# Emptying a PSUM bank before the score copies, and one P@V visit for tiles that span two batches

## The chip, the core and the metric

The kernel runs on one core of one Trainium2 chip. The metric is the device time of one execution in microseconds (us); the median of several runs counts. The engines are called as the profile calls them: PE (TensorE's matmuls) with PEld (its weight loads), DVE (VectorE), ACT (ScalarE), POOL (GpSimd) and SP (SyncE, which here only issues DMAs).

## What is computed

Attention in which each query keeps its 32 largest scores, and behind it a feed-forward layer with the activation h cos h:

```python
# q, k, v: (8 batches, 8 heads, 576 tokens, 64)
scores = scale * np.matmul(q, k.transpose(0, 1, 3, 2))
kth = np.partition(scores, -32, axis=-1)[..., -32:-31]
scores = np.where(scores >= kth, scores, -1e9)
scores = scores - np.max(scores, axis=-1, keepdims=True)
attn = np.exp(scores)
attn = attn / (np.sum(attn, axis=-1, keepdims=True) + 1e-09)
x = np.matmul(attn, v)          # then as (4608 tokens, 512)
h = x @ w_in                    # w_in: 512 x 2048
out = (h * np.cos(h)) @ w_out   # w_out: 2048 x 512
```

All of it is float32.

## The kernel before

**Tiles, units, slots, blocks.** The 4608 tokens are cut into 36 tiles of 128. A tile with one pair of heads is a *unit*; four pairs make 144 units, four for each tile. As a batch has 576 tokens, that is 4.5 tiles, four of the tiles (the fifth of each nine) span two batches: 64 of their rows belong to one batch and 64 to the next, and they need the k and v of both. The main loop has one *slot* for each unit (`slot`, L724), and each engine's instructions are written in the order in which the slots are written. I call the slots of a *block* (the four of a tile) slot 0 to slot 3, after i mod 4.

**One unit's way.** It is a software pipeline. Scores are made by PE one or two slots ahead, in slots 0 and 2 for two units each (`scores`, L229): 448 columns into a bank `sc`, the last 128 into parts of a shared PSUM tile `rim`. ACT copies both parts to SBUF (`take_scores`, L246 and L250). In slot i, DVE folds the row of unit i in two halves (L258), with POOL making the lower half (L274, L283), and searches the top 32 (L350 MAX8, L355 MATCH_REPLACE8). In slot i + 1 the bounds of this search (L363, L370) go to ACT, which masks (L377, L379) and takes exponentials (L387, with the denominators accumulated); DVE sums and inverts the denominators (L395, L400). In slot i + 2 POOL splits the weights into 16-bit halves (L410, L412), and SP writes them to DRAM (`rows`, L438) and reads them back transposed (`pT`, L444).

**P@V.** `values` (L469) multiplies pT by v into `rim`, for several units in one *visit*. Which slot has the visit of which unit is set by `value_slot` (L672). An ordinary tile has one visit for its four units, in slot 2 of the next block. A spanning tile has two visits: units 0 and 1 in slot 0 of the next block, units 2 and 3 in slot 2. After a visit DVE multiplies by the inverted denominators and writes xT (`take_values`, L481). xT, L250 and P@V all touch `rim`, and L250 in a slot with a visit waits for the visit's end, as xT waits for that L250.

**Feed-forward.** `ff1` (L530) is the input projection: eight items for a block, and two of them, a *pair*, fill one PSUM bank (`mm`). ACT empties a full bank twice, into g (L544) and x (L546); POOL reduces the argument (L566, L575), ACT takes the sine (L585, with its own table load), POOL multiplies (`gate`, L592). `ff2` (L605) is the output projection, eight items that all add up in one other bank; ACT empties it (L615) and sends it out. The two banks `mm` are the only ones, so with the output projection in one, all pairs go through the other in turn.

**The order by hand.** `plan` (L717) says for each of the four slots which feed-forward items come at its three feeds (0 is an ff1 item, 1 an ff2 item): the first feed stands before the scores and P@V of the slot, the second and third behind. `take_banks` (L552) writes the emptying of the banks that are complete by then, where it is called; in a slot this was between the mask and the exponentials (L758), and again behind the second feed (L773). The block's first pair of ff1 items is in slot 3: with the plan before, its first item is in the first feed and its second in the second feed.

**Loads.** SP issues the loads of q, k and v. `load_at` (L690) puts at most one load in a slot, at the earliest in the slot where the last reader of its buffer stands. The pool `loads` has six buffers each for q, k and v.

Of the kernel before, what the change touches and what calls it, by code (L numbers as in the profile page):

```python
# [10 lines left out]
F32 = mybir.dt.float32  # L11
# [6 lines left out]
P = 128  # L18
# [12 lines left out]
def kernel(  # L31
# [13 lines left out]
    NT = S // P  # L45
    TAIL = S - NT * P
    MAIN = NT * P
    NP = H // 2
# [6 lines left out]
    consts = ctx.enter_context(tc.tile_pool(name="consts", bufs=1))  # L55
    loads = ctx.enter_context(tc.tile_pool(name="loads", bufs=6))
    work = ctx.enter_context(tc.tile_pool(name="work", bufs=2))
    small = ctx.enter_context(tc.tile_pool(name="small", bufs=4))
    ps = ctx.enter_context(tc.tile_pool(name="ps", bufs=2, space=bass.MemoryType.PSUM))
    dram = ctx.enter_context(tc.tile_pool(name="dram", bufs=4, space=bass.MemoryType.DRAM))  # L60
    ffw = ctx.enter_context(tc.tile_pool(name="ffw", bufs=2))
# [41 lines left out]
    def load_weights(n, queue):  # L103
        for _ in range(n):
            i = wq["next"]
            if i >= len(chunks):
                return
            src, dst = chunks[i]
            if not DECODE:
                queue.dma_start(out=dst, in_=src)  # L110
                wq["next"] = wq["done"] = i + 1
                continue
            spare = i < 2 * NC + 10 and i % 2 == 1 and staged(1) < XB
            if spare:
                st = ffw.tile([P, CW, 2], I32, tag="x", name="st", bufs=XB)
            elif staged() + ff["live"] >= CHUNKS:
                return
            else:
                st = ffw.tile([P, CW, 2], I32, tag="g", name="st", bufs=CHUNKS)
            queue.dma_start(out=st.rearrange("p w i -> p (w i)"), in_=src)  # L120
            wq["loaded"].append((st, dst, int(spare)))
            wq["next"] = i + 1
# [16 lines left out]
    def decode_second(n):  # L139

        for _ in range(min(n, len(wq["second"]))):
            st, w, spare = wq["second"].popleft()
            wi = w.bitcast(I32)
            nc.vector.tensor_scalar(
                out=wi, in0=wi, scalar1=3, scalar2=None, op0=ALU.logical_shift_left
            )
            wq["third"].append((st, w, spare))
# [14 lines left out]
    for t0 in range(0, B * S, P):  # L162
        parts = []
# [14 lines left out]
    def place(hp, j):  # L178

        return (hp + j) % 2  # L180
# [23 lines left out]
    def load_v(b, hp):  # L204
        st = pairs.setdefault((b, hp), {})
        cols = slice(hp * P, (hp + 1) * P)
        t = loads.tile([P, NT, P], F32, tag="v", name="v")
        nc.sync.dma_start(out=t, in_=v[b, 0:MAIN, cols].rearrange("(c p) e -> p c e", p=P))
        st["v"] = t

        t = st["v_tail"] = v_tails[b % 2 * NP + hp]
        for j in range(2):
            nc.sync.dma_start(
                out=t[place(hp, j) * TAIL : (place(hp, j) + 1) * TAIL],
                in_=v[b, MAIN:S, hp * P + j * D : hp * P + (j + 1) * D],
            )
# [61 lines left out]
    def fold_low(u):  # L278

        if u["n"] in BUSY:  # L280
            return
        low = u["low"].bitcast(I32)
        nc.gpsimd.tensor_tensor(  # L283
            out=low, in0=low, in1=u["rest"][:, :, HS:S].bitcast(I32), op=ALU.subtract
        )

    dens = []
    for i in range(3):
        t = consts.tile([P, 2, 2], F32, tag=f"dens{i}", name=f"dens{i}")
        nc.vector.memset(t[:, :, 1], EPS)  # L290
        dens.append(t)

    tops = []
    for i in range(3):
        t = consts.tile([P, 2, TOPK + 1, 2], F32, tag=f"top{i}", name=f"top{i}")
        nc.vector.memset(t[:, :, 0, 1], -NEG)
        tops.append(t)
# [3 lines left out]
    def topk_first(u, w):  # L301

        u["top"] = tops[u["n"] % len(tops)]
        if w:
            merge_first(w)
        if u["n"] not in BUSY:
            fold_sum(u)
        fold_high(u)
        if w:
            merge_second(w)  # L310
        if u["n"] in BUSY:
            fold_now(u)
        topk_round(u, 0, [lambda: bounds(w), lambda: distances(w)] if w else ())

    def topk_round(u, rnd, between=(), ahead=None):
        top, rest, lasts = u["top"], u["rest"], TOPK // 8 - 1
        end = TOPK - 1 - 8 * rnd
        at = top[:, :, end : end - 8 if rnd < lasts else None : -1, 0]
        search(
            at, rest[:, :, HS:S] if rnd == 0 else rest[:, :, 0:HS], rest[:, :, 0:HS], rnd < lasts,  # L320
            between if rnd < lasts else (),
        )
        if rnd < lasts:
            return
        del u["rest"]
        low = u.pop("low")
        for k in range(TOPK // 16):
            more = k < TOPK // 16 - 1
            if ahead and not more:
                take_values(ahead)  # L330
            search(top[:, :, 1 + 8 * k : 9 + 8 * k, 1], low, low, more, () if more else between)
# [51 lines left out]
    def exponentials(u):  # L383
        s, nd = u["s"], u.pop("nd")
        den = u["den"] = dens[u["n"] % len(dens)]
        for j in range(2):
            nc.scalar.activation(  # L387
                out=s[:, j], in_=s[:, j], func=AF.Exp, bias=nd[:, j : j + 1], scale=SCALE,
                accum_out=den[:, j, 0:1],
            )  # L390
# [57 lines left out]
    def place_of(u):  # L448

        bank, at = u["hp"] % 2, u["hp"] // 2 * P  # L450
        return bank, room[bank][:, at : at + P]
# [23 lines left out]
    def take_values(us):  # L475
        blk, hp, n = block_of[us[0]["tok"]], us[0]["hp"], len(us)
        if "xT" not in blk:
            blk["xT"] = work.tile([P, NP, P], F32, tag="xT", name="xT", bufs=3)
        for i, u in enumerate(us):
            to, o, pT = blk["xT"][:, hp + i], place_of(u)[1], u.pop("pT")  # L480
            nc.vector.tensor_tensor(out=to, in0=o, in1=pT[:, 2 * NT + 1], op=ALU.mult)  # L481
        blk["left"] -= n
        blk["tick"] = ff["tick"]
# [5 lines left out]
    for w in widths:  # L489
        blk = {"t0": t0, "w": w, "left": 0, "g": [], "gated": []}  # L490
# [61 lines left out]
    def take_banks():  # L552
        while full:
            take, *what = full.popleft()
            take(*what)
# [116 lines left out]
    def value_slot(i, u):  # L672

        if i < NP:
            return NP + 1
        return i - i % NP + NP + (0 if len(u["parts"]) == 2 and u["hp"] < 2 else 2)

    valued = {}
    for i, u in enumerate(units):
# [1 line left out]
    scored, last, last_values = {}, {}, {}  # L681
# [8 lines left out]
    def load_at(i, *what):  # L690
        while i in at_slot:
            i += 1
        at_slot[i] = what

    order = [(b, hp) for b in range(B) for hp in range(NP)]
    for n in range(NP, len(order)):
        i = last[order[n - 6]] if n >= 6 else 0
        load_at(max(i, 2 * NP + 2), load_qk, *order[n])
        i = last_values[order[n - 6]] if n >= 6 else 0
        load_at(max(i, 2 * NP + 2), load_v, *order[n])  # L700

    for hp in range(NP):
# [8 lines left out]
    def send(x):  # L711
# [6 lines left out]
        ((0, 0), (1,), (1,)),  # L718
        ((0, 0), (1, 1), (0,)),
        ((0,), (1,), ()),  # L720
        ((1, 0), (0, 1), (1,)),
    )

    def slot(i, u, w, x, z):  # L724
        n = (3, 4, 4, 4, 4, 3)[i] if i < NP + 2 else 2
        if i < NP:
            for load, b, hp in at_once[i]:
                load(b, hp)
        load_weights(n, nc.sync if i < NP + 2 else nc.scalar)
        if x:  # L730
            (turn if i < NP + 2 else send)(x)
        decoding = i < 3 * NP
        ff["late"] = False
        topk_first(u, w)
        fold_low(u)
        topk_round(u, 1)
        topk_round(u, 2)
        if i > 0:
            decode_second(NP)
            decode_third()  # L740
        reduce_first()
        reduce_second()
        made = scored.get(i, [])
        if z:
            take_banks()
        feed(*plan[i % NP][0])

        for m in made:
            scores(m)
        if z:  # L750
            values(z)


        if i % 2 or decoding:
            sines(1)
        if w:
            mask(w)
        take_banks()  # L758
        if w:
            exponentials(w)  # L760
        if i + 1 < NU:
            take_scores(units[i + 1])
        topk_round(u, 3, both(w), z)
        if i == 0:
            decode_second(NP)
            decode_third()
        ff["late"] = True
        if i in at_slot:
            load, b, hp = at_slot[i]
            load(b, hp)  # L770
        gate(1)
        feed(*plan[i % NP][1])
        take_banks()  # L773
        decode_first(NP)
        reduce_first()
        reduce_second()
        feed(*plan[i % NP][2])
# [40 lines left out]
    for i in range(NU):  # L818
        ff["now"] += 1
        wq["ready"] = wq["done"]  # L820
        u, w, x = (units[i - n] if n <= i else None for n in range(3))
# [46 lines left out]
```

## Time and profile before

| | |
|---|---|
| median of 3 runs (lowest, highest) | 1444.02 us (1443.61, 1445.5) |
| profiled execution | 1442.98 us |
| its span, first to last instruction | 1441.2 us |
| mean granted PE clock, whole span | 0.984 |
| PE, DVE, POOL, ACT busy | 95%, 94%, 81%, 76% |
| HBM traffic | 101 GB/s |

How to read the views. The page gives the busy time of each engine and, as digits, its busy share in 40 equal slices. The timeline lists instructions by their start: start, duration, engine, line, operation, what is written from what, how many equal ones follow each other, and in brackets the engine's idle time before them with what ended it. A row of matmuls in float32 counts two records for each matmul; their ends are modelled, so for PE starts are compared with starts. A window line gives busy times of the engines in a stretch. Before 110 us the granted PE clock was 0.83, from 280 us on it was 1.00. The weights are decoded in the first 110 us.

### The profile page before, as it was taken

The page shows a single profiled execution, that of the slowest core. Times are in us where ns is not written, and L with a number is a line of the kernel's source. Part 1 is how long each engine was busy: PE and PEld are TensorE (multiplying, and loading weights), DVE is VectorE, ACT ScalarE, POOL GpSimd, SP SyncE. Part 2 cuts the span into 40 slices and gives each one's busy share as a digit, 9 for nine tenths or more (in the row PEclk, how much of TensorE's full clock was granted, in tenths as well). Part 3 has the DMA queues.
Part 4 walks back from the last instruction along what each step waited for, and adds up shares of the span by engine and source line. Part 5 has one row for each costly group of instructions (what it writes and reads, how often), then busy time and mean ns, then how long its engine had stood idle before and what let it go on. Part 6 is the DMA issues. An engine that isn't in the chain of part 4 may idle for free.

```text
span 1441.2 us, 30374 instructions
## 1 busy us (share of the span) xinstructions
PE 1376.0 (95%) x10304; PEld 993.1 (69%) x10304; DVE 1352.8 (94%) x5235; ACT 1091.4 (76%) x1922; POOL 1167.5 (81%) x804
## 2 busy tenths in 40 slices
PE   5558999999999999999999999999999999999998
PEld 3446677777777767777777767777777776777775
DVE  8999999999999999999999999999999999999931
ACT  7877777777877777778777787877777778777741
POOL 4878888888888887888888888888888888888820
PEclk9688999999999999999999999999999999999999
DMA  9576766566665566556665666657666566565630
GB/s 296 181 217 175 185 190 173 151 170 188 163 176 148 160 187 171 167 146 194 171 187 141 143 185 182 173 139 186 187 162 165 151 170 155 151 160 148 154 99 15
DMA packets 427437, 240.02 MB, mean 167 GB/s; under 512 B 375952, under 2 KB 392592, under 8 KB 427280
## 3 DMA queue, kind: packets, MB, share of 16 engines
q1 hardware_dynamic: 420720, 224.22, 57.8%
q10 hardware_dynamic: 6560, 13.85, 2.7%
q8 instruction: 81, 1.33, 0.4%
q14 instruction: 76, 0.62, 0.1%
HBM read 45.09 MB, written 101.19 MB: 101 GB/s over the span
## 4 chain that ended last, share of the span: by engine, by line
PE 63%; ACT 19%; DVE 16%; issue 1%; POOL 1%; POOLq 0%
PE mm L530 26%; PE o L605 18%; PE rim L469 10%; PE sc L236 7%; DVE top L350 7%; ACT s L387 4%; ACT L387 3%; ACT s L379 3%; ACT s L246 2%; DVE rest L355 2%; DVE rest L258 2%; DVE xT L481 2%; PE rim L236 2%; ACT x L546 2%; ACT s L250 2%; ACT g L544 1%
## 5 line engine op out<-in xcount | busy, mean ns | idle before, releaser
L530 PEld LDWEIGHTS mm<-xT,w_in 128*128 128x128 f32 x4608 | 535.8, 192 | 97.4 <-issue 49.1
L530 PE MATMUL mm<-xT,w_in 128*128 128x128 f32 x4608 | 543.5, 276 | 18.0 <-ACT x L546 14.6
L605 PE MATMUL o<-w_out,g 128*128 128x512 f32 x1152 | 524.7, 599 | 0.0
L350 DVE MAX8 top<-rest 128x8 f32<-128x288 f32 x1152 | 478.8, 451 | 0.0
L355 DVE MATCH_REPLACE8 rest<-top,rest 128x288 f32<-128x288 f32 x864 | 376.5, 443 | 0.0
L605 PEld LDWEIGHTS o<-w_out,g 128*128 128x128 f32 x1152 | 207.7, 190 | 217.8 <-issue 210.5
L410 POOL COPY halves<-s 128x2304 uint16<-128x2304 uint16 x140 | 294.8, 2106 | 76.0 <-ACT s L387 75.9
L350 DVE MAX8 top<-low 128x8 f32<-128x288 f32 x576 | 241.8, 448 | 0.6 <-POOL low L283 0.6
L387 ACT ACTIVATE s<-s,nd 128x576 f32<-128x576 f32 x288 | 220.4, 769 | 0.8
L283 POOL TENSOR_TENSOR low<-low,rest 128x576 int32<-128x576 int32 x141 | 199.4, 1414 | 11.1
L379 ACT ACTIVATE s<-s,top 128x576 f32<-128x576 f32 x288 | 205.6, 761 | 0.0
L274 POOL TENSOR_TENSOR low<-s 128x576 int32<-128x576 int32 x141 | 199.0, 1411 | 6.0 <-ACT s L250 6.0
L377 ACT ACTIVATE nd<-nd 128x2 f32<-128x2 f32 x144 | 29.4, 204 | 207.0 <-DVE nd L370 207.0
L575 POOL TENSOR_TENSOR x<-g,x 128x1024 f32<-128x1024 f32 x68 | 161.2, 2371 | 5.7
L592 POOL TENSOR_TENSOR g<-g,x 128x1024 f32<-128x1024 f32 x68 | 160.9, 2366 | 0.0
L236 PE MATMUL sc<-k,q 64*128 64x448 f32 (+1 forms) x640 | 148.7, 587 | 11.6 <-DMA k<-in_k_dram 6.2
L469 PE MATMUL rim<-pT,v 128*64 128x128 f32 (+1 forms) x2560 | 139.9, 267 | 0.0
L469 PEld LDWEIGHTS rim<-pT,v 128*64 128x64 f32 x2560 | 129.7, 139 | 7.1 <-issue 6.0
L246 ACT COPY s<-sc 128x896 f32<-128x896 f32 x144 | 128.3, 891 | 3.2 <-PE sc L236 3.1
L355 DVE MATCH_REPLACE8 low<-top,low 128x288 f32<-128x288 f32 x288 | 125.4, 443 | 0.0
L544 ACT ACTIVATE g<-mm 128x512 f32<-128x512 f32 x144 | 85.4, 593 | 48.1 <-PE mm L530 47.6
L258 DVE TENSOR_TENSOR rest<-sc,s 128x576 f32<-128x576 f32 x144 | 107.8, 749 | 10.5 <-ACT s L250 10.3
(54 smaller groups left out, 1236.1 us busy)
## 6 DMA issues: line engine op xcount, KB each, us to landing
rows<-halves SPq DMA_DIRECT2D x140, 640.0 KB, 3.0
out_dram<-ob ACTq DMA_DIRECT2D x36, 256.0 KB, 2.1
q<-in_q_dram SPq DMA_DIRECT2D x31, 288.0 KB, 3.5
st<-in_moe_w_in_dram SPq DMA_DIRECT2D x16, 512.0 KB, 6.1
v<-in_v_dram SPq DMA_DIRECT2D x32, 256.0 KB, 3.2
k<-in_k_dram SPq DMA_DIRECT2D x31, 144.0 KB, 3.3
k<-in_k_dram SPq DMA_DIRECT2D x32, 128.0 KB, 3.6
st<-in_moe_w_out_dram SPq DMA_DIRECT2D x8, 512.0 KB, 4.3
```

The lines of the kernel that those rows point to most:

```text
L236: nc.tensor.matmul(to[r0 : r0 + rows, rim_bank(r0, j) if k0 else place(u["hp"], j), 0 : k1 - k0], st["q"][d, q0 : q0 + rows], st["k"][d, k ...
L274: nc.gpsimd.tensor_tensor(out=u["low"].bitcast(I32), in0=s[:, :, 0:HS], in1=s[:, :, HS:S], op=ALU.add)
L283: nc.gpsimd.tensor_tensor(out=low, in0=low, in1=u["rest"][:, :, HS:S].bitcast(I32), op=ALU.subtract)
L350: nc.vector.max(to[:, j], src[:, j])
L355: nc.vector.match_replace(rest[:, j], to[:, j], src[:, j], NEG)
L379: nc.scalar.activation(out=s[:, j], in_=s[:, j], func=AF.Prelu, bias=less[:, j, 1:2], scale=1.0, alpha=FAR)
L387: nc.scalar.activation(out=s[:, j], in_=s[:, j], func=AF.Exp, bias=nd[:, j : j + 1], scale=SCALE, accum_out=den[:, j, 0:1],)
L410: nc.gpsimd.tensor_copy(out=halves[:, :, 0 : 2 * S], in_=s.rearrange("p (k h) -> p h k", h=2))
L469: nc.tensor.matmul(to[d, r], lhsT, rhs, start=(bank, j) not in begun, stop=c == NT - 1 and u in us[-2:] and r0 + rows == P,)
L530: nc.tensor.matmul(mm[:, at : at + w], w_in[f // FC][:, c, (f % FC) * P : (f % FC + 1) * P], blk["xT"][:, c], start=c == 0, stop=c == NC - 1,)
L575: nc.gpsimd.tensor_tensor(out=x, in0=g, in1=x, op=ALU.subtract)
L605: nc.tensor.matmul(o, g[:, at : at + P], w_out[f], start=f == 0, stop=f == NF - 1)
```

## The change

Nothing is computed differently. The plan gives both items of a block's first pair to the first feed of slot 3, and the two output items behind them to the second feed. In slot 3, banks are no longer emptied between the mask and the exponentials, but between the exponentials and the score copies; the new call has nothing to do in the other slots, where the one ahead of the exponentials has just emptied all. A spanning tile's four units get one visit of P@V, in slot 2 of the next block as all others. As v of both batches is then needed by all four pairs at once, v has eight buffers instead of six, and its loads are placed by the reader eight loads back. To make room, four kinds of small tiles lose a buffer: those of the pool `small` (4 to 3), `dens` and `tops` (3 to 2 each) and xT (3 to 2).

```diff
-    small = ctx.enter_context(tc.tile_pool(name="small", bufs=4))
+    small = ctx.enter_context(tc.tile_pool(name="small", bufs=3))
...
-        t = loads.tile([P, NT, P], F32, tag="v", name="v")
+        t = loads.tile([P, NT, P], F32, tag="v", name="v", bufs=2 * NP)
...
     dens = []
-    for i in range(3):
+    for i in range(2):
...
     tops = []
-    for i in range(3):
+    for i in range(2):
...
-            blk["xT"] = work.tile([P, NP, P], F32, tag="xT", name="xT", bufs=3)
+            blk["xT"] = work.tile([P, NP, P], F32, tag="xT", name="xT", bufs=2)
...
-        return i - i % NP + NP + (0 if len(u["parts"]) == 2 and u["hp"] < 2 else 2)
+        return i - i % NP + NP + 2
...
-        i = last_values[order[n - 6]] if n >= 6 else 0
+        i = last_values[order[n - 2 * NP]] if n >= 2 * NP else 0
         load_at(max(i, 2 * NP + 2), load_v, *order[n])
...
-        ((1, 0), (0, 1), (1,)),
+        ((1, 0, 0), (1, 1), ()),
...
         if w:
             mask(w)
-        take_banks()
+        if i % NP != 3:
+            take_banks()
         if w:
             exponentials(w)
+        take_banks()
         if i + 1 < NU:
             take_scores(units[i + 1])
```

## The prediction

> **What bounds the kernel now.** I read the page's first two parts, then the idle times slot by slot, then the timeline of one steady block. The page has two engines near full:
>
> ```profile
> PE 1376.0 (95%) x10304; PEld 993.1 (69%) x10304; DVE 1352.8 (94%) x5235; ACT 1091.4 (76%) x1922; POOL 1167.5 (81%) x804
> PE   5558999999999999999999999999999999999998
> DVE  8999999999999999999999999999999999999931
> ```
>
> DVE has next to no idle before about 110 us, PE almost none after it, and the last 76 us (1365 to 1441) are PE's alone. So from 114 us on I ask what PE waits for. Part 4's chain agrees (PE 63%). The wait that ends last there is found by comparing two stretches with the same work on PE's timeline, eight rows of output projection and 32 of input projection, each ended by score matmuls:
>
> ```profile
> 598.00 3.60 PE L605 MATMUL o<-w_out,g 128*128 128x512 f32 x8
> 601.44 3.73 PE L530 MATMUL mm<-xT,w_in 128*128 128x128 f32 x32
> 605.11 1.02 PE L236 MATMUL sc<-k,q 64*128 64x448 f32 x4
> ...
> 618.60 3.60 PE L605 MATMUL o<-w_out,g 128*128 128x512 f32 x8
> 622.29 3.84 PE L530 MATMUL mm<-xT,w_in 128*128 128x128 f32 x32
> 626.06 1.02 PE L236 MATMUL sc<-k,q 64*128 64x448 f32 x4
> ```
>
> From o to scores the first takes 605.11 - 598.00 = 7.11 us (7.10 in nanoseconds), the second 7.46. The 0.36 is a stall. It sits in slot 3 of the block, before the second pair of the next block's input projection, and its releaser is ACT's L546. ACT's timeline of that slot says why:
>
> ```profile
> 619.25 0.76 ACT L387 ACTIVATE s<-s,nd 128x576 f32<-128x576 f32 x1
> 619.92 0.19 ACT L387 ACTIVATION_READ_ACCUMULATOR s<-s,nd 128x1 f32 x1
> 620.01 0.89 ACT L246 COPY s<-sc 128x896 f32<-128x896 f32 x1
> 620.79 0.37 ACT L250 COPY s<-rim 128x256 f32<-128x256 f32 x1
> 621.06 0.60 ACT L544 ACTIVATE g<-mm 128x512 f32<-128x512 f32 x1
> 621.55 0.69 ACT L546 ACTIVATE x<-mm,quarter 128x512 int32<-128x512 f32 x1
> ```
>
> The first pair's bank was complete at 615.03 + 3.73 = 618.76, yet L544 and L546 empty it only after both score copies, until 622.24. PE goes on at 622.29.
>
> PE's delay comes back to DVE once a block, because the xT products follow P@V:
>
> ```profile
> 612.02 0.88 DVE L481 TENSOR_TENSOR xT<-rim,pT 128x128 f32<-128x128 f32 x4 [0.46 <-ACT s L250]
> 622.86 0.75 DVE L258 TENSOR_TENSOR rest<-sc,s 128x576 f32<-128x576 f32 x1
> ```
>
> L250 in that slot itself waits for P@V's end (1.43 us). The 0.46 is all the idle time that DVE has in a steady block. A block takes 37.31 us: DVE works 36.85 of it. PE's pieces, from start to start, are 7.11 + 7.10 + 2.15 (scores) + 7.11 + 7.10 + 2.15 + 4.24 (P@V) = 36.96 without the stall. PE is the longer one by 0.11.
>
> **Bank emptied earlier.** On ACT, four instructions change places in slot 3; nothing is added, no table load moves, and PE's and POOL's orders there stay as they are (the changed plan only moves the seam between two feeds, with no scores or P@V between them). L544 starts at 620.01 instead of 621.06; L544 and L546 took 622.24 - 621.06 = 1.18, so the bank is free at 621.19 and PE can go on at 621.24, and as it needs 0.11 from release to its first matmul (3.84 against 3.73 us for 32), at 621.35. Unstalled it would get there at 618.60 + 3.44 = 622.04. The stall goes with 0.69 to spare. That distance holds in the new rhythm too, since in slot 3 both sides hang on P@V's end in slot 2: DVE by xT, PE by its order. What is late next: P@V for xT again, with 0.46 - 0.36 = 0.10 of DVE idle left.
>
> The price: the two score copies end at 622.24 instead of 621.16. Their next reader is DVE's L258 at 622.86 (0.62 of cover), then POOL's L274 at 623.17; PE's scores overwrite that bank after 626. Where the copied unit is the first of a spanning tile, L250 comes as two (0.74 instead of 0.37) and the cover is 0.25. So I cost it at nothing. Without cover it would be up to 1.18 a block.
>
> How often: I took the o-to-scores time of slot 3 for each block. 20 steady blocks show 7.46: 20 x 0.36 = **7.2 us**. Around each of four spanning tiles three blocks show 7.96, 7.98 and 7.93: 0.86 + 0.88 + 0.83 = 2.57, x 4 = **10.3 us** (a later start of ACT there, and the second L250). The block at 126.49 shows 8.57, a stall of 1.47; its exponentials end at 129.00, so PE is let go at 129.00 + 1.18 + 0.16 = 130.34 against 129.93 unstalled and 0.41 stays. Of the other 1.06 part is lost at once, since P@V at 154.15 waits for a landing pT. Ends 0 and 1.06; I take **0.5**. The long stall in slot 7 (6.09 us) is before 114 us, where PE waits for DVE and ACT anyhow: nothing, although the bank there is emptied after the exponentials and so later.
>
> **One visit of P@V for spanning tiles.** Before, units 0 and 1 of such a tile were visited in the next slot 0, units 2 and 3 in slot 2:
>
> ```profile
> 554.65 3.70 PE L605 MATMUL o<-w_out,g 128*128 128x512 f32 x8
> ...
> 555.17 0.49 DVE L481 TENSOR_TENSOR xT<-rim,pT 128x128 f32<-128x128 f32 x2 [0.71 <-ACT s L250]
> ...
> 566.10 0.16 DVE L395 TENSOR_REDUCE den<-dens 128x2 f32<-128x4 f32 x1 [1.08 <-ACT s L387]
> ```
>
> The early visit runs 551.93 to 554.65, 2.71 us; the later one (571.00) also 2.71. The merged visit has the same 160 records of the same form. No row shows one; the nearest say 5.42 for the sum of the two, and 4.24 for an ordinary visit with half the records. I take 5.42 since the 64-wide rows are issued every 0.032 us whatever stands around them; the low end would give another 4 x 1.2 = 4.7. So PE gains nothing here directly. What goes is the wait of L250 and xT in slot 0 (0.71) and what follows from PE's lag in slot 1: L544 waiting 2.03 for PE, L395's 1.08, POOL's 3.9. What comes is P@V ending 5.42 - 4.24 = 1.18 later in slot 2. L250, xT and ACT's sine load queue behind that, and DVE idles about 1.3 there. PE waits for none of these: o needs g gated 8 us earlier, and the next xT reader stands behind 3.5 us of o. The 10.3 above rests on this, as slots 0 and 1 of such tiles then look like ordinary ones.
>
> **Buffers.** Two tiles for top and dens instead of three: a slot's first MAX8 overwrites what ACT's L379 read in the slot before. That ends at 617.17, MAX8 comes 6.4 us later. Two xT: the overwritten one was last read four slots earlier. small with three: read a slot later. All nothing; they cost only if ACT fell 6 us behind. The v loads move on SP: some earlier at the start, around spanning tiles by about two slots later. Each lands in 3.2 us and is needed slots later. A v load waits for the visit that frees its buffer, and behind it on SP stand the next slot's rows write and transpose. The merged visit ends about 7.97 + 1.18 = 9.15 us into a slot of 11.5, the rows write comes at 0.4 of the next: 2.7 us of cover, and another 3.3 between the transpose's landing and P@V.
>
> **Sum.** 7.2 + 10.3 + 0.5 = 18.0. The profiled execution took 1442.98 (span 1441.2 and 1.8 around it): 1425.0. The median of the runs, 1444.02, is 1.04 above it: **1426.0 us**.
>
> **A rule against it.** The Trainium skill (Perfetto Trace Analysis, Identifying the Most-Contended Engine) tells TensorE's headroom by the share of weight loads, not by matmul time, and wants the engine of highest occupancy treated first. For one steady block:
>
> ```profile
> 280.00:317.32 37.32, 37.23 (x275) 26.94 (x274) 36.86 (x145) 29.19 (x52) 32.44 (x23) 1.00 0.58 165
> ```
>
> (columns: PE, PEld, DVE, ACT, POOL busy and counts, clock, DMA). By the rule PE is at 26.94 / 37.32 = 72% and DVE at 99%. Then PE's stall is free and all of DVE's idle can go: 20 x 0.46 + 4 x (0.46 + 3.15 + 0.27) + 2.1 near the start = 26.8, giving 1417. The rows say that the 28% is no headroom: an o matmul takes 0.43 us for one load of 0.19. I keep PE's 36.96 as the floor.
>
> **Rivals.**
> - The merged visit brings its own wait (0.12). If ACT's later sine, or a v or pT, stalls PE by 1.5 us a tile, 6 of the 10.3 are lost: 1432. For it: visits did hang on a pT once (154.15). Against: the 3.3 us of slack elsewhere.
> - DVE alone bounds (0.05): 1417, as worked out.
> - The stall moves (0.09): PE, freed, waits for something that DVE or POOL paces, and steady blocks keep their 37.3. The bank might also not be emptied earlier if L544 waited for PE; the bank was complete 1.25 us before. Only part of the tiles' 10.3 stays: 1434 to 1444.
> - Slower (0.06): the moved score copies reach L258 late. Its place is DVE's start of slot 0; with no cover the price is 1.18 a block, so DVE takes 38.03 instead of today's 37.31: 33 x 0.72 = 24 us less the tiles' 10: 1458. It decides once ACT's exponentials in slot 3 end over 0.62 + 0.46 us later than in the trace, which a late sine could do. Against it: ACT waits 1.18 for DVE there.
>
> **Chances.** The forecast (1423.5 to 1428.5) has 0.68. Slower or faster by 0.2%, 2.9 us, is about what a measurement here can tell from no change. Faster: 0.68 + 0.12 + 0.05 + 0.05 of the third = 0.90; within: 0.04; slower: 0.06. The range 1422 to 1434 holds the forecast, the first rival and a third of the moved stall.
>
> **What would show it.** Right: o to scores is 7.10 in every slot 3, the L546 wait of PE's L530 is gone after 130 us, xT's wait in steady blocks is about 0.1, blocks take 36.96, tiles have one 160-record visit of about 5.4 us. Wrong: idle time before L258 in slot 0, a PE wait of over 0.1 us in another slot, or xT's wait still 0.46.

## The result, and the profile after

| | before | after |
|---|---|---|
| median (lowest, highest), 4 runs each | 1443.95 us (1443.61, 1445.5) | 1422.62 us (1422.21, 1423.78) |
| profiled execution | 1442.98 us | 1422.95 us |
| its span | 1441.2 us | 1421.2 us |

The ratio of after to before is 0.9852, with a 95% interval of 0.9834 to 0.9869: 1.5% faster. The prediction's 1426.0 is 3.4 too high. The result lies inside its range (1422 to 1434), but 0.9 below the narrower forecast of 1423.5 to 1428.5 that had 0.68 of the chances.

The page of after, its line of busy times and the first line of its chain:

```profile
PE 1365.5 (96%) x10304; PEld 993.8 (70%) x10304; DVE 1351.6 (95%) x5233; ACT 1086.1 (76%) x1922; POOL 1166.0 (82%) x804
...
PE 92%; DVE 6%; ACT 1%; POOL 0%; DMA 0%; issue 0%; POOLq 0%
```

The busy shares have hardly moved. What has moved is the chain: PE was 63% of it, with 19% of ACT and 16% of DVE between; now it is PE's work from end to end but for the first 112 us and one transfer of pT at 148 us. That is how a stall that was removed shows in a kernel of which two engines were nearly full; the chain's shares move far more than the time, which fell by 1.5%.

The stall itself, in PE's timeline of a slot 3 (start, duration, engine, line, what is written from what, how many):

```profile
609.84 3.60 PE L605 MATMUL o<-w_out,g 128*128 128x512 f32 x8
613.28 3.73 PE L530 MATMUL mm<-xT,w_in 128*128 128x128 f32 x32
616.94 1.02 PE L236 MATMUL sc<-k,q 64*128 64x448 f32 x4
```

From o to scores it is 616.94 - 609.84 = 7.10, where it was 7.46. I took that distance for each block: from the second block on it is 7.10 in all of them, also around the spanning tiles; the first has 7.39. What exceeds 7.10 adds up to 0.29, where it was 18.92 before.

ACT's timeline of the same slot:

```profile
611.15 0.19 ACT L387 ACTIVATION_READ_ACCUMULATOR s<-s,nd 128x1 f32 x1
611.24 0.57 ACT L544 ACTIVATE g<-mm 128x512 f32<-128x512 f32 x1
611.72 0.67 ACT L546 ACTIVATE x<-mm,quarter 128x512 int32<-128x512 f32 x1
612.29 0.90 ACT L246 COPY s<-sc 128x896 f32<-128x896 f32 x1
613.08 0.39 ACT L250 COPY s<-rim 128x256 f32<-128x256 f32 x1
```

The bank is free at 612.39, and PE, which gets to its second pair at 613.28, finds it so. The price: the score copies end at 613.47, and DVE's L258 starts at 614.09. The cover is 0.62, as forecast: L258 starts 2.75 after the end of the exponentials (611.34), as it did before the change (622.86 - 620.11). L258 itself has no idle time before it.

One steady block (busy time and count of PE, PEld, DVE, ACT and POOL, then clock, DMA share, GB/s):

```profile
273.00:309.98 36.98, 36.98 (x274) 27.04 (x273) 36.87 (x146) 29.06 (x51) 32.40 (x23) 1.00 0.60 166
```

PE has no gap in it. The window is 0.02 longer than a block: from one slot 3 to the next PE takes 36.96 (starts of L605 at 276.57 and 313.53), where it took 37.31. DVE has 0.11 of idle time, the wait of xT, which was 0.46. (The timeline prints no idle time as short as 0.11; it is the distance between the two records.)

The merged visit of a spanning tile, on PE's timeline:

```profile
560.97 0.46 PE L469 MATMUL rim<-pT,v_tail 64*64 64x64 f32 x16
561.36 2.08 PE L469 MATMUL rim<-pT,v 128*64 128x64 f32 x64
563.37 0.46 PE L469 MATMUL rim<-pT,v_tail 64*64 64x64 f32 x16
563.76 2.09 PE L469 MATMUL rim<-pT,v 128*64 128x64 f32 x64
565.78 3.70 PE L605 MATMUL o<-w_out,g 128*128 128x512 f32 x8
```

It takes 565.78 - 560.97 = 4.81, in each of the four tiles, not 5.42. And DVE behind it:

```profile
566.30 0.88 DVE L481 TENSOR_TENSOR xT<-rim,pT 128x128 f32<-128x128 f32 x4 [0.30 <-ACT s L250]
```

This 0.30 and a 0.59 four slots earlier are all that DVE waits around a tile.

**Where the 20.0 of span came from.** 7.2 from 20 steady blocks; 10.3 from the three blocks around each tile; 4 x 0.61 = 2.4 from the visits; in the first block 8.57 - 7.39 = 1.18, of which 0.58 went back at the next P@V (5.14 instead of 4.56, where it waits 0.52 for a landing pT); and PE's first P@V started 0.3 later. Sum: 7.2 + 10.3 + 2.4 + 0.6 - 0.3 = 20.2.

### The profile page after: what moved, and what is told of

Same layout as the page of the kernel before. It is cut to its first block, busy times and chain, and to the rows that moved or that the text cites. A ratio compares the mean times of both kernels' runs of the same rounds, so it can differ in the third digit from the quotient of the medians.

```text
span 1421.2 us, 30370 instructions
## 1 busy us (share of the span) xinstructions
PE 1365.5 (96%) x10304; PEld 993.8 (70%) x10304; DVE 1351.6 (95%) x5233; ACT 1086.1 (76%) x1922; POOL 1166.0 (82%) x804
## 4 chain that ended last, share of the span: by engine, by line
PE 92%; DVE 6%; ACT 1%; POOL 0%; DMA 0%; issue 0%; POOLq 0%
PE o L605 36%; PE mm L530 35%; PE rim L469 11%; PE sc L236 8%; DVE top L350 3%; PE rim L236 2%; DVE rest L355 1%; DVE rest L258 0%; DVE low L355 0%; DVE w_in L144 0%; DMA pT<-rows 0%; DVE w_out L144 0%; ACT s L387 0%; PE warm L813 0%; ACT s L379 0%; POOL w_out L154 0%
## 5 line engine op out<-in xcount | busy, mean ns | idle before, releaser
L605 PE MATMUL o<-w_out,g 128*128 128x512 f32 x1152 | 524.7, 599 | 0.0
L605 PEld LDWEIGHTS o<-w_out,g 128*128 128x128 f32 x1152 | 207.7, 190 | 218.0 <-issue 214.2
L566 POOL TENSOR_SCALAR x<-x 128x1024 f32<-128x1024 int32 x68 | 71.3, 1048 | 61.4 <-ACT x L546 61.4
L258 DVE TENSOR_TENSOR rest<-sc,s 128x576 f32<-128x576 f32 x144 | 107.7, 748 | 7.0 <-ACT s L250 6.8
```

The source lines that it names most:

```text
L605: nc.tensor.matmul(o, g[:, at : at + P], w_out[f], start=f == 0, stop=f == NF - 1)
```

## The experiments

My theory: two independent gains. The bank's earlier emptying ends every stall of slot 3, those of the tiles too; PE is the bound there, and anything that DVE still waits is hidden. The merged visit adds 0.61 a tile on PE directly. The prediction had it otherwise, and is the first rival: the tiles' 10.3 hang on the merged visit. Each ratio is to the kernel before, run on the same chip.

| run | median us | before there | ratio (95%) |
|---|---|---|---|
| e1_bank_only | 1424.75 | 1442.47 | 0.987 (0.9853 to 0.9887) |
| e2_visit_only | 1438.5 | 1442.47 | 0.9973 (0.9961 to 0.9985) |
| e3_buffers_only | 1442.59 | 1442.47 | 1.000 (0.999 to 1.001) |
| e4_bank_earlier | 1421.65 | 1442.47 | 0.9857 (0.9837 to 0.9877) |
| e5_no_tail | 1412.2 | 1442.51 | 0.978 (0.9764 to 0.9796) |
| e6_tails_first | 1420.8 | 1442.51 | 0.984 (0.9823 to 0.9856) |
| e7_one_copy_late | 1426.81 | 1442.51 | 0.9881 (0.9862 to 0.9901) |
| e8_two_copies_late | 1459.21 | 1442.51 | 1.0105 (1.0087 to 1.0123) |
| e9_less_dve | 1422.96 | 1443.36 | 0.9855 (0.9842 to 0.9869) |
| e10_tails_first_again | 1421.19 | 1443.36 | 0.9843 (0.9829 to 0.9856) |
| e11_after_again | 1423.06 | 1443.36 | 0.9857 (0.9843 to 0.9871) |

For e5 to e8 I take 0.9857 (the ratio of e11) x 1442.51 = 1421.9 as the changed kernel's time on that chip; it is an estimate, as the changed kernel was not run beside them.

### The two parts alone, and the buffers

e1 is the kernel before with the bank's part only:

```diff
-        ((1, 0), (0, 1), (1,)),
+        ((1, 0, 0), (1, 1), ()),
...
-        take_banks()
+        if i % NP != 3:
+            take_banks()
         if w:
             exponentials(w)
+        take_banks()
```

> The bank's emptying alone (changed plan for slot 3, bank emptied between exponentials and score copies); spanning tiles keep two visits of P@V, all pools as before. Theory (PE bounds from 114 us on, and every stall of slot 3 is ACT's order alone): all stalls of slot 3 go, those around spanning tiles too, since in those slots too the bank is complete before ACT's exponentials end: 7.2 + 10.3 + 0.5 = 18 us less, 1426, and o to scores is 7.10 in every slot 3 after 130 us; DVE keeps idle times of about 3 us a tile in slots 0 and 1 of the block behind a spanning tile. Rival (as the prediction's text had it: the tiles' 10.3 rests on the merged visit): only 0.36 of each of the tiles' stalls goes, 7.2 + 12 x 0.36 + 0.5 = 12 us less, 1432.

It takes 17.7 less. The stalls are gone in all blocks but the first (7.90). Slot 3 behind a tile's two visits shows it. In the kernel before, PE waited there, and from o (580.83) to scores (588.75) it took 7.92:

```profile
584.98 3.84 PE L530 MATMUL mm<-xT,w_in 128*128 128x128 f32 x32 [0.56 <-ACT x L546]
```

In e1 the same slot:

```profile
573.02 3.60 PE L605 MATMUL o<-w_out,g 128*128 128x512 f32 x8
576.46 3.73 PE L530 MATMUL mm<-xT,w_in 128*128 128x128 f32 x32
580.12 1.02 PE L236 MATMUL sc<-k,q 64*128 64x448 f32 x4
```

This is 7.10, and so are the two slots 3 ahead of it. DVE two slots earlier, in slot 1 of the same block:

```profile
558.29 0.16 DVE L395 TENSOR_REDUCE den<-dens 128x2 f32<-128x4 f32 x1 [1.00 <-ACT s L387]
559.35 0.76 DVE L258 TENSOR_TENSOR rest<-sc,s 128x576 f32<-128x576 f32 x1 [0.27 <-ACT s L250]
```

These waits of the split visits are still there (1.00 for L395, which was 1.08); only the 0.71 of xT in slot 0 has gone. PE goes through slot 3 in 7.10 all the same. So the tiles' 10.3 come from the bank; the prediction's reason for them falls.

e2 is the kernel before with all buffers and one visit:

```diff
-        return i - i % NP + NP + (0 if len(u["parts"]) == 2 and u["hp"] < 2 else 2)
+        return i - i % NP + NP + 2
```

> One visit for spanning tiles alone, with eight buffers for v and the smaller pools; plan and emptying of banks as before. Theory (PE's row is what counts): the visit takes 4.81 instead of 2 x 2.71, 0.61 less a tile, and of the three stalls around a tile only the last falls from 0.83 to 0.36 (it comes from DVE's lag behind the early visit; the other two come from the second L250): 4 x (0.61 + 0.47) = 4.3 us less, 1439.7; steady blocks stay at 37.31 with 0.46 of idle before xT. Rival (what DVE idles counts): DVE's 3.15 and 0.27 of idle at each tile fall to the 0.46 of a steady block each: 4 x 2.5 = 10 us less, 1434.

It takes 4.0 less: the tiles lose 0.61 each in the visit (4.81) and about 0.5 in one of their three stalls (7.95, 7.97 and now 7.45). In e2 the wait behind the merged visit is longer than in the changed kernel:

```profile
572.29 0.89 DVE L481 TENSOR_TENSOR xT<-rim,pT 128x128 f32<-128x128 f32 x4 [1.14 <-ACT s L250]
```

The 1.3 that the prediction gave this wait is about right here, where PE still has its stall; in the changed kernel, without the stall, it is the 0.30 above. e1's 17.7 and e2's 4.0 make 21.7; the changed kernel was 20.3 (beside e11) and 21.3 (in the first comparison) below the kernel before. About 2 of e2's 4.0 are part of stalls that e1 ends too, so some shortfall is due; it is no larger than what these runs differ by.

e3 is e2 without the line above, so it has the buffers alone.

> The buffers alone (v with eight, small with three, dens, tops and xT with two; v loads placed by the reader eight loads back); two visits, plan and banks as before. Theory: no wait is added and none removed, 1444 within 2 us, stalls of slot 3 as before. Rival (the earlier v loads in the first 60 us, or a waiting top or xT, matter): over 3 us either way, with an idle time of DVE before L350 or of PE before L530 that was not there.

There is no difference, as the prediction had costed them.

### The bank emptied a step earlier still

e4 leaves the old call in slot 3 and so empties the bank between mask and exponentials, with the changed plan:

```diff
-        if i % NP != 3:
-            take_banks()
+        take_banks()
```

> The changed kernel, but in slot 3 too banks are emptied between mask and exponentials, so ACT waits there for the first pair's last matmul. Rival (ACT's order sets the pace: in the trace of the changed kernel ACT would wait 1.6 us there, so the exponentials and the score copies come that much later, 1.0 over the cover of L258): about 1.0 us more a block, 33 x 1.0 less 0.1, 1452. Theory (PE is the longer engine by 0.11 a block, and a DVE that is late once gives PE a lead that makes the first pair complete earlier, after which ACT no longer waits): one transient of some 1 us, behind each spanning tile another fraction, steady blocks back at 36.96: 1423 to 1427, with DVE's idle time no longer before xT but before L258 or L395, about 0.1 a block.

It takes 1421.65, as the changed kernel does. L544 waits 0.68 for PE there, the exponentials start later by that and the 1.2 of the bank, and yet nothing is lost. All stalls are gone, the first one too, and the 0.11 that DVE waits in a block stands before L258 instead of xT. The trace of the changed kernel had let me expect a wait of 1.6 for L544. That it is only 0.68 fits a PE that has moved ahead of ACT; this is read from one trace, and no run takes that lead away. So of the two places tried, both ahead of the score copies, neither is seen to be better.

The profiled execution of e4 alone was 4.5 longer than the median, by one visit at 114 us that took 9.50 instead of 5.23. Of this, 1.57 was a wait for a late pT; most of the rest is the granted clock, 0.55 over that visit where it was 0.79 in the trace of after.

### Is PE the floor?

e5 takes work from PE, e9 from DVE.

```diff
-            for c in (NT, *range(NT)):
+            for c in range(NT):
```

> The changed kernel without the v_tail matmuls of P@V: the last 64 keys of every batch are left out of P@V, so the output differs there. Each visit of 80 records loses its 16 v_tail ones (2 x 0.28), so PE's pieces fall from 36.96 to about 36.36 a block (two merged tile visits' worth less in the tiles), below the 36.85 that DVE works. Theory (after the change PE and DVE are 0.11 a block apart, so PE has next to nothing more to give): DVE becomes the bound, blocks take 36.86 to 36.87, xT's idle time goes to 0; gain 33 x 0.11 = 3.6, at most DVE's 7.8 of idle time, plus 0.6 to 1.2 at the end where PE is alone: 7 less at most, 1414 to 1418 where the changed kernel has 1421. Rival (PE alone sets the time): 36 visits x 0.6 = 22 less, 1400.

It takes 9.7 less, over the 7 that the theory allowed at most, but far from 22. A block of e5, and the first line of its chain:

```profile
278.36:315.11 36.75, 36.62 (x258) 26.51 (x257) 36.75 (x146) 28.82 (x51) 32.31 (x23) 1.00 0.59 167
```

```profile
DVE 91%; PE 5%; ACT 2%; issue 1%; POOL 1%; POOLq 0%
```

DVE is without a gap, and PE waits again for L546 (7.5 from o to scores) at no cost. What the theory had too small is DVE's distance: its block is 36.75, not 36.87. So 33 x (36.96 - 36.75) = 6.9; the tiles' longer visits, 4.81 - 4.24 = 0.57 each, go behind DVE: 2.3; the two last visits, in PE's tail, are 0.38 shorter each: 0.8. That is 10.0, and it loses 1.2 for the first block's stall, which is back (8.57). The sum is 8.8 of the 9.7.

```diff
-            search(top[:, :, 1 + 8 * k : 9 + 8 * k, 1], low, low, more, () if more else between)
+            search(top[:, :, 1 + 8 * k : 9 + 8 * k, 1], low, low, more and u["n"] < 12, () if more else between)
```

> The changed kernel, from unit 12 on without the two MATCH_REPLACE8 and their loads on low (left out: the step that takes the first eight values out of low before the next eight are sought, so the lower half of the top-k list differs). DVE gets 4 x 0.86 = 3.4 a block less to do: 33.4 instead of 36.87. Theory (in the changed kernel PE's 36.96 is the floor of a block): blocks stay at 36.96, DVE only waits more for P@V; 0 to 2 less than the changed kernel. Rival (the engine with the highest share of busy time, DVE with 99% of a block, sets the time): 33 x 3.4 = 113 less, or what part of it PE's loads, 73%, let go.

It takes 1422.96 beside 1423.06 for the changed kernel on the same chip (e11). One of DVE's waits, and the window of about one block, of e9:

```profile
297.48 0.16 DVE L395 TENSOR_REDUCE den<-dens 128x2 f32<-128x4 f32 x1 [1.36 <-ACT s L387]
```

```profile
275.00:312.00 37.00, 37.00 (x275) 27.06 (x274) 33.77 (x129) 29.21 (x52) 32.34 (x23) 1.00 0.59 166
```

DVE has 3.1 less to do in this window (36.87 to 33.77, for much the same stretch) and waits that much more; PE is gapless, as before. 104 us of DVE's busy time were taken out (1351.6 to 1247.5) and the kernel is no faster: in the changed kernel PE's row of matmuls is the floor.

### How far the score copies may slip

e7 puts one more copy of the scores in front of the two in slot 3, e8 two (`range(2)`):

```diff
-        s = u["s"] = work.tile([P, 2, S], F32, tag="s", name="s", bufs=4)
+        s = u["s"] = u["s"] if "s" in u else work.tile([P, 2, S], F32, tag="s", name="s", bufs=4)
...
+        if i % NP == 3 and i + 1 < NU:
+            units[i + 1]["s"] = work.tile([P, 2, S], F32, tag="s", name="s", bufs=4)
+            for _ in range(1):
+                nc.scalar.copy(out=units[i + 1]["s"][:, :, 0:SB], in_=units[i + 1]["sc"][:, :, 0:SB])
         if i + 1 < NU:
             take_scores(units[i + 1])
```

> The changed kernel with one extra score copy (L246, 0.78 from start to start) ahead of the two of slot 3, so that they reach DVE's L258 0.78 later. The prediction gave them 0.62 of cover. Theory: L258 waits 0.16 to 0.2 in each block; DVE takes 36.86 + 0.18 = 37.04 where PE needs 36.96: 33 x 0.08 = 2.6, and some 1 to 2 more at the tiles' second L250: 2 to 6 us more than the changed kernel. Rival (PE's lead or DVE's order absorbs it, as where the bank was emptied between mask and exponentials): no change. Rival (there was no cover): 33 x 0.67 = 22 more.

> As with one extra score copy, but two (1.56 later). Theory: L258 waits 0.94 to 1.0 in each block, DVE takes 37.82 where PE needs 36.96: 33 x 0.86 = 28, 28 to 36 us more than the changed kernel, that is 1449 to 1457: the slower case of the prediction from its deciding point on. Rival (absorbed): no change.

They take 4.9 and 37.3 more than the changed kernel. The extra copy cost 0.93, not 0.78; in e7, ACT and then DVE:

```profile
613.17 0.90 ACT L766 COPY s<-sc 128x896 f32<-128x896 f32 x1
614.10 0.91 ACT L246 COPY s<-sc 128x896 f32<-128x896 f32 x1
614.90 0.38 ACT L250 COPY s<-rim 128x256 f32<-128x256 f32 x1
```

```profile
615.31 0.76 DVE L258 TENSOR_TENSOR rest<-sc,s 128x576 f32<-128x576 f32 x1 [0.26 <-ACT s L250]
```

and in e8:

```profile
324.17 0.76 DVE L258 TENSOR_TENSOR rest<-sc,s 128x576 f32<-128x576 f32 x1 [1.19 <-ACT s L250]
```

Both give the same cover: 0.93 - 0.26 = 0.67 and 2 x 0.93 - 1.19 = 0.67, for the 0.62 that I read as the distance of two records. DVE pays for every delay beyond that. Its blocks are 37.10 in e7, 0.14 over PE's 36.96, and 38.04 in e8, 1.08 over it. On PE, nine blocks with one tile among them take 333.27 in after (239.62 to 572.89), 334.41 in e7 and 342.83 in e8; for 33 blocks that is 4.2 and 35 more. The slower rival is thus real: beyond 0.67 of delay DVE pays, and from about 0.8 on (0.93 - 0.14 and 1.86 - 1.08, an estimate), when the 0.21 by which PE's block is the longer is used up, the time does.

### Half the switches once more

The visit is 0.61 shorter than two of 2.71, with the same records. In e1 the split visit's four stretches start at 563.20, 563.47, 564.55 and 564.83, so v_tail x8 takes 0.27 and v x32 1.08. Of the merged visit, x16 takes 0.39 and x64 2.01. Twice the records cost 0.12 and 0.93 more. So a tail record takes 0.015 and one of v 0.029, and each stretch has some 0.15 beside its records. e6 sets both tails first, so that a visit has two stretches instead of four:

```diff
-        for b, _, rows, r0 in us[0]["parts"]:
-            r = slice(r0, r0 + rows)
-            for c in (NT, *range(NT)):
+        for cs in ((NT,), range(NT)):
+            for c, (b, _, rows, r0) in [(c, part) for part in us[0]["parts"] for c in cs]:
+                r = slice(r0, r0 + rows)
                 for u in us:
```

> The changed kernel, with the v_tail matmuls of both parts of a spanning tile's visit issued first and then the v ones of both, so that the visit goes once from 64-wide to 128-wide matmuls and not twice; same 160 records. Theory (what the merged visit gained beyond the records is a fixed cost at each such change of form, some 0.15 to 0.3): the visit takes 4.5 to 4.65 instead of 4.81, 0.6 to 1.2 us less in all. Rival (the time goes by the count of records alone): 4.81, no change.

> The kernel with the v_tail matmuls of both parts first, once more, beside the changed kernel on one chip. Theory (0.30 a visit less, 1.2 in all): 1.2 less than the changed kernel, up to 2.5 if the first block's P@V meets its pT earlier too. Rival (no change beyond the traces): within 0.3 of it.

PE's timeline of e10:

```profile
560.37 0.69 PE L469 MATMUL rim<-pT,v_tail 64*64 64x64 f32 x32
561.00 3.95 PE L469 MATMUL rim<-pT,v 128*64 128x64 f32 x128
564.88 3.70 PE L605 MATMUL o<-w_out,g 128*128 128x512 f32 x8
```

The visit takes 4.51 in all four tiles of both runs: 0.30 less for two stretches less, as expected, and x32 and x128 (0.63 and 3.88) fit the same 0.15.

> The changed kernel as it is, as the measure for the other two: 1421 to 1423 if its ratio to the kernel before, 0.985, repeats.

Side by side it is 1421.19 against 1423.06, that is 1.9 less, of which 1.2 are the visits. The other 0.7 is in the first 160 us: P@V at 152.6 waited 0.43 for a pT and took 5.06, against 1.16 and 5.79 in e11, and this differs between executions of one kernel (5.14 in the first profile of after). Only the 1.2 is shown by the traces; the intervals of the two ratios overlap.

## Why the prediction was right

- **The stall in slot 3 and its cause: right.** Undone, it is back (e2); done alone, it is gone (e1). 7.2 from steady blocks, as forecast.
- **The tiles' 10.3: right in size, wrong in reason.** "The 10.3 above rests on this", the merged visit. It rests on the bank (e1). The step that failed: I saw DVE's and ACT's waits in slots 0 and 1 of a tile and took it that the later start of ACT would outlast the earlier emptying. In e1 the waits of slot 1 are there and PE is not late. That the 10.3 came out although its reason was wrong is luck. No run shows the first rival's wait of PE behind the merged visit either.
- **The merged visit at 5.42: mis-sized.** It measured 4.81, so "PE gains nothing here directly" was 2.4 short. I had the bounds, 4.24 and 5.42, and chose the upper end because each record would take 0.032 wherever it stands. The rows give 0.015 for a tail record and 0.029 for one of v; the rest of the 5.42 are the changes between tails and full rows, 0.15 each, and merging halves them from eight stretches to four.
- **First block, 0.5: not settled.** The trace of after has 0.6: part of the gain was lost at once to a landing pT, and the stall left was 0.29 for 0.41. That the figure fits is in part luck. In e11, the same kernel, the first stall is 0.58 (7.68) and P@V behind it takes 5.79 instead of 4.56, so 0.89 - 1.23 = -0.3. The term is no larger than what executions differ by.
- **Profiled against median.** Of the 3.4 by which 1426.0 is too high, 2.05 is the sum against the profiled execution (1425.0 for 1422.95); the rest is that I put the median 1.04 above the profiled time, and after it is 0.33 below. The merged visit's 2.4, at nothing in the sum, is the largest term that was missed; with it the sum would have been 1423.6.
- **Score copies at nothing: right**, and the cover that I read (0.62) measured 0.67 (e7, e8). The price without cover was also right in kind: I put the deciding point at 0.62 + 0.46 = 1.08 later; a delay of 0.93 is still faster than before and one of 1.86 slower, 1459. By these two, a steady block is back at its old 37.31 with a delay of 0.8 + 0.35, about 1.15 (an estimate).
- **PE's floor: right, the distance to DVE too small.** PE's 36.96 is the block that was measured. DVE was not 0.11 behind it but 0.21: the 36.85 of busy time was 36.75 once DVE did not wait (e5).
- **The rule against it.** The Trainium skill (Perfetto Trace Analysis, Identifying the Most-Contended Engine) judges TensorE's headroom by MFU (its share of the peak arithmetic) and by the busy share of weight loads, and has the most occupied engine optimized first. The prediction used the weight loads alone: with PE at 72% and DVE at 99%, that gave 1417. The runs don't agree with it. e9 takes 104 us of work from DVE and gains nothing, e5 takes work from PE and gains until DVE binds. In this kernel the rows decided: matmuls back to back, start to start. But DVE is close behind, and the next microseconds have to be taken from both.

The first blocks differ from run to run for two reasons that the traces show. P@V at 114 us has the same records in after and e7, and its length follows the granted clock (the second number from the left is the length, the third from the right the clock):

```profile
114.50:119.72 5.22, 5.22 (x82) 4.72 (x80) 5.22 (x21) 3.12 (x7) 1.93 (x2) 0.79 0.44 151
114.04:120.12 6.08, 6.08 (x82) 5.58 (x80) 5.46 (x21) 3.12 (x7) 2.78 (x3) 0.68 0.54 160
```

Length times clock is 5.22 x 0.79 = 4.12 in after and 6.08 x 0.68 = 4.13 in e7. P@V at 153 us waits for a landing pT, 0.52 in after and 1.16 in e11. What sets the moment at which the clock rises or the pT lands is open, and so are 0.9 of e5's 9.7.

## What to carry to other kernels

When two engines are almost equally full, compare stretches of equal work on the one whose pieces, from start to start, sum to the block's length; the difference is the stall, and the instruction that releases it says whose order to change. Before counting on a second part of a change for the first part's gain, ask whether the waits that it removes are on the bound engine at all. A step that is moved back has a cover that can be read as the gap between its end and its reader's start; it is then worth knowing how thin it is, since here it was 0.67 us, and a delay of 1.86 us turned 1.5% faster into 1% slower.

## What the runs showed of the hardware

- A stretch of 64-row v_tail matmuls or of 128-row v ones, with a change from the other form ahead of it, costs PE about 0.15 beyond its records: 0.27, 0.39 and 0.63 for 8, 16 and 32 tail records, 1.08, 2.01 and 3.88 for 32, 64 and 128 of v (e1, after, e10).
- A wait lengthens DVE's slot by about 0.09 more than its idle column says. With no wait a slot 0 is 8.99 and a slot 2 is 9.78 (e5). With 0.11 of xT's wait (after) slot 2 is 9.99, with 0.26 before the next L258 (e7) slot 3 is 9.33 instead of 8.99, with 1.19 (e8) it is 10.26. So DVE's own work in a block is 3 x 8.99 + 9.78 = 36.75, not the 36.85 that busy time gives.
- Two copies into the same tile of scores on ACT were 0.93 apart from start to start (e7), while a copy followed by one into another part took 0.79 (after). Why is not shown.
- The visit of P@V at 114 us took 4.71 in e1, 5.22 in after and 6.08 in e7, at a mean granted clock over it of 0.89, 0.79 and 0.68. Length times clock is 4.1 to 4.2 in all three.
